# Attention and a routed expert layer on one core: weight splits in two pieces in place of eight, and four early tiles in place of three

## The chip, the cores and the metric

The kernel runs on one core of one Trainium2 chip. Its time is the device time of one execution in microseconds (us). Before the change three executions were timed. One more execution was profiled; its trace is what the profile's views are read from. A core has five engines that run their own instruction streams side by side: PE (matrix multiply), ACT and DVE (element-wise work), POOL (element-wise work and indirect transfers) and SP (which here only issues transfers). An engine's streams are tied together by semaphores: an instruction can wait until another engine has finished a certain number of its own.

## The reference

Attention comes first (8 batches, 8 heads, head size 64, 512 local and 32 global tokens), then a layer of eight experts of which each token uses one:

```python
# local tokens see local tokens within 32 positions and all 32 global ones; global tokens see all
s_ll = np.where(np.abs(pos[:, None] - pos[None, :]) <= 32, scale * q_l @ k_l.T, -1e9)
a_l = softmax(concat([scale * q_l @ k_g.T, s_ll]))
x = concat([out_g, out_l], axis=2)          # -> 8 x 544 = 4352 rows of 512
...
e_idx = np.argmax(x @ w_gate, axis=1)       # one of 8 experts a row
gate_w = softmax(x @ w_gate)[row, e_idx]
eom = sigmoid(x @ w_output_gate)
h = np.maximum(x[mask] @ w1[e], 0.0)        # w1[e]: 512 x 1024
out[mask] = gate_w * eom[mask, e] * (h @ w2[e])   # w2[e]: 1024 x 512
```

Which rows go to which expert is known only once attention has run.

## The kernel before, in words

**Attention and routing.** Units of attention pass through a pipeline (`advance`), a unit being a pair of heads for half of a batch's local tokens, or a part of its global ones. As rows become complete, a router writes each row with its gate factor and its number into a table `xd` in memory, and works out from the experts' counts a list of row numbers that is sorted by expert.

**Early tiles.** A tile is 128 rows of one expert. Expert 0's weights are loaded and split while attention still runs. So the first `KPRE` = 3 tiles of expert 0 that can be filled from the first 25 of 34 row tiles are worked on inside the tail of attention and of the routing arithmetic. `fetch_pre` gathers their rows (POOL), `turn_pre` transposes them (SP), `pre1` and `pre2` are the two matrix stages, `pre1_out` and `pre2_out` what follows them. They are cut into chunks that `work(n)` puts between other instructions; `work_all` runs those that are left, just before the expert slots.

**Expert slots.** The rest of the rows go through slots of one tile each. The number of tiles that the experts need is known only on the chip. `NBASE` = 36 slots always run (`run(0, NBASE)`); further ones stand in a tail block that is entered only if they are needed (`rest`, in steps of 2 and 3). A slot s is made of

- `gather(s)`: POOL fetches the rows (L1040), five slots ahead;
- `xtrans(s)`: a transposing DMA that SP issues (L1046), four slots ahead;
- `stage1(s)`: 96 matmuls on PE (L668), two slots ahead. Numbers are kept as sums of a high and a low half-precision part, so each product is taken as high x high, low x high and high x low, and the weights exist as `w1h` and `w1l`;
- `between(s)`: ACT takes the positive part (L674) and DVE its low part (L675);
- `stage2(s)`: 24 matmuls (L679) with `w2h` and `w2l`;
- `store(s)`: ACT scales by the gate factor (L682) and POOL scatters the rows to the output (L683).

**Changes of expert.** Where a slot is the first of a new expert, its weights, 2 MB for each matrix, must be in `w1h`/`w1l` and `w2h`/`w2l`. SP fetches the raw weights under a condition (L1012, L1014) as soon as the old raw ones are used up. Then ACT makes the high part and DVE the low part: `split1` (L693 and L695) for w1, `split2` (L699 and L701) for w2, each in eight pieces f of 512 elements a partition. Whether to do so is decided on the chip: `change` holds a Switch of two arms, one of them empty (L1019), and `changes(s)`, which runs behind each slot's stage 2, one of four (L1028): nothing, w1 for slot s + 3, w2 for slot s + 1, or both.

```python
for arm in tc.Switch(flag, 4):
    for which in (1, 2):
        if arm & which:
            for f in range(8):
                (split1 if which == 1 else split2)(f)
```

ACT and DVE each read the flag from a table, jump into an arm and come back behind the Switch. Around a Switch the count that other engines wait for must come out the same whatever arm was run, so an arm that leaves work out adds what is owed.

The order on each engine is the order in which the code is written. Nothing reorders it.

Of the kernel before, what the change touches and what calls it, by code (L numbers as in the profile page):

```python
# [21 lines left out]
S = SL + SG  # L22
# [5 lines left out]
RPE = NT  # L28
KPRE = 3
G0, G1 = (4, 7)  # L30
# [13 lines left out]
NSLOT = NT + E - 1  # L44
NBASE = NSLOT - 5
XG = DM + 8
# [12 lines left out]
def tile_attention_moe(  # L59
# [69 lines left out]
    def load_v(b, i):  # L129
        raw[i] = ld.tile([P, VW], F32, name="vf", bufs=5)  # L130
        nc.sync.dma_start(raw[i], vD[b, :, i])
# [104 lines left out]
    nc.sync.dma_start(xd[0:1, :], zrow[0:1])  # L236
    w1h = [wst.tile([P, 4, P], F16, name=f"w1h{f}") for f in range(8)]
    w1l = [wst.tile([P, 4, P], F16, name=f"w1l{f}") for f in range(8)]

# [449 lines left out]

    def split1(f, hi=True, lo=True):  # L690
        src = w1r[:, :, f * P:(f + 1) * P]
        if hi:
            nc.scalar.mul(w1h[f], src, WS)  # L693
        if lo:
            nc.vector.scalar_tensor_tensor(w1l[f], src, WS, w1h[f], ALU.mult, ALU.subtract)  # L695

    def split2(f, hi=True, lo=True):
        if hi:
            nc.scalar.mul(w2h[f], w2r[:, f], WS)  # L699
        if lo:  # L700
            nc.vector.scalar_tensor_tensor(w2l[f], w2r[:, f], WS, w2h[f], ALU.mult, ALU.subtract)  # L701

# [31 lines left out]
    def fetch_pre():  # L734
        for t in range(KPRE):
            x = ld.tile([P, XROW], F32, name="kf", bufs=3)
            gp.indirect_dma_start(out=x, out_offset=None, in_=xd[0:1 + NPRE * P, :],
                                         in_offset=bass.IndirectOffsetOnAxis(ap=ixp[:, t:t + 1], axis=0))
            pre[t] = {"x": x}
        pre_at.append(n)  # L740

    def turn_pre():
        for t in range(KPRE):
            xT = ld.tile([P, S], F32, name="qf", bufs=3).bitcast(F16)[:, 0:2 * DM].rearrange("p (k t) -> p k t", t=P)
            nc.sync.dma_start_transpose(out=xT, in_=pre[t]["x"].bitcast(F16)[:, 0:2 * DM])
            pre[t]["xT"] = xT
# [23 lines left out]
    def pre2_out(t):  # L770
        d = pre[t]
        y = ld.tile([P, VW], F32, name="vf", bufs=5)[:, 0:DM]
        s2_out(d["py"], y, d["x"])
# [242 lines left out]
    def change(s, which):  # L1016

        flag = {ET.Activation: entry(nc.scalar, 0, s), ET.DVE: entry(nc.vector, 0, s)}
        for arm in tc.Switch(flag, 2):  # L1019
            if arm == 1:  # L1020
                for f in range(8):
                    (split1 if which == 1 else split2)(f)
        fetch(s, which)

    def changes(s):

        flag = {ET.Activation: entry(nc.scalar, 4, s, 3), ET.DVE: entry(nc.vector, 4, s, 3)}
        for arm in tc.Switch(flag, 4):  # L1028
# [37 lines left out]
    def run(lo, hi, grouped=True):  # L1066

        for s in range(lo, hi):
# [13 lines left out]
            store(s, grouped)  # L1082

    for s in range(5):
        gather(s)
    for s in range(2):
        xtrans(s)
    fetch(-1, 1)
    fetch(-1, 2)
    xtrans(2)  # L1090
    for s in range(2):
        change(s, 1)
        stage1(s)
        between(s)
    xtrans(3)
    changes(-1)
    run(0, NBASE)

    def rest(lo, sizes):
# [5 lines left out]
        for arm in tc.Switch(more, 2):  # L1105
            if arm == 1:
                for s in range(lo, hi):
                    gather(s)
                for s in range(lo, hi):
                    xtrans(s)  # L1110
                for s in (lo, lo + 1):
                    change(s, 1)
                    stage1(s)
                    between(s)
                if hi > lo + 2:
                    changes(lo - 1)
                else:
                    change(lo, 2)
# [78 lines left out]
```

## Time and profile before

| | us |
|---|---|
| median of 3 runs | 746.26 (745.1 to 753.59) |
| profiled execution, its own time | 746.95 |
| its span on the core | 745.1 |
| PE busy | 686.4 (92%) |
| PE weight loads (beside PE) | 525.4 (71%) |
| DVE busy | 379.4 (51%) |
| ACT busy | 377.3 (51%) |
| POOL busy | 240.4 (32%) |

The mean clock that PE was granted is 0.974 of full speed. In the rows below, "x" ahead of a number is a count of instructions, `L668` a line of the kernel, and `out<-in` the operands by the program's names (`qkv` is the large buffer that attention used and that the expert slots use again, for raw w2, its split parts and the rows of the slots). What stands in square brackets, or behind the second bar of a group, is the time in which the engine stood idle just before the instruction, and what ended it; `ACTq` or `DVEq` is that engine's sequencer, where a branch or a count is meant and not an operation, and "issue" is a wait for nothing that the trace shows.

### The profile page before, as it was taken

To read this page: it belongs to the slowest core of one execution; us is meant where nothing else is said; L and a number is where in the kernel's file an instruction comes from. 1 tells how busy PE (TensorE), PEld (TensorE's weight loads), DVE (VectorE), ACT (ScalarE), POOL (GpSimd) and SP (SyncE) were. 2 spreads that over 40 slices of the span, in tenths; PEclk is the share of its full clock that TensorE was granted. 3 is DMA by queue.
4 is the path that set the end of the run, shared out by engine and by line. 5 is a ranking of instruction groups with operands and counts; after the bars stand their busy time and mean duration, and the time that the engine had idled before them with its cause. 6 is when DMAs were issued, how large, how long until landed. Compare 5 with 4: busy or idle time off the path is not lost.

```text
span 745.1 us, 23135 instructions
## 1 busy us (share of the span) xinstructions
PE 686.4 (92%) x9042; PEld 525.4 (71%) x9042; DVE 379.4 (51%) x1110; ACT 377.3 (51%) x866; POOL 240.4 (32%) x335
## 2 busy tenths in 40 slices
PE   4999999999999989947999899999999998999991
PEld 3788887878788777647667577667776775776660
DVE  3798989898998976710333410134225251343200
ACT  3788889898899994101342411133235262243210
POOL 3335374664748464320112121111211212121110
PEclk9999999999999999978999999999999999999996
DMA  7764979678677784297548573365765978652110
GB/s 229 226 168 127 293 213 287 148 243 208 161 236 157 208 159 75 101 264 144 168 141 221 112 149 90 81 173 124 166 189 124 238 170 212 163 113 65 49 44 14
DMA packets 113797, 120.18 MB, mean 161 GB/s; under 512 B 81615, under 2 KB 83407, under 8 KB 111762
## 3 DMA queue, kind: packets, MB, share of 16 engines
q1 hardware_dynamic: 106898, 96.85, 51.2%
q0 software_dynamic: 6528, 19.67, 9.2%
q14 instruction: 295, 2.42, 1.2%
q8 instruction: 76, 1.25, 0.7%
HBM read 200.50 MB, written 19.42 MB: 295 GB/s over the span
## 4 chain that ended last, share of the span: by engine, by line
issue 47%; PE 27%; POOL 10%; DVE 8%; ACT 4%; DMA 1%; SPq 1%; POOLq 1%; DVEq 0%; ACTq 0%
PE sp L256 6%; POOL out_dram L683 5%; POOL qkv L1040 4%; PE pt L303 3%; PE pt L308 3%; PE sp L365 2%; DVE dl L324 2%; PE sp L668 1%; DMA qkv<-in_kT_dram 1%; DVE nm L267 1%; PE pt L394 1%; DVE fl L316 1%; PE sp L261 1%; PE po L421 1%; ACT qkv L709 1%
## 5 line engine op out<-in xcount | busy, mean ns | idle before, releaser
L668 PE MATMUL ph<-qkv,w1h 128*128 128x128 f16 x2304 | 203.9, 222 | 15.1 <-DMA qkv<-qkv 10.0
L668 PEld LDWEIGHTS <-w1h 128*128 128x128 f16 x2496 | 197.0, 100 | 24.0 <-issue 10.5
L668 PE MATMUL ph<-qkv,w1l 128*128 128x128 f16 x1152 | 200.8, 222 | 9.3 <-DVEq L1028 4.1
L679 PE MATMUL py<-qkv 128*128 128x512 f16 x864 | 192.0, 379 | 0.0
L675 DVE SCALAR_TENSOR_TENSOR qkv<-ph,qkv 128x512 f16<-128x512 f32 x72 | 46.8, 687 | 213.1 <-ACT qkv L674 120.6
L679 PEld LDWEIGHTS <-qkv 128*128 128x128 f16 x896 | 86.0, 98 | 97.1
L668 PEld LDWEIGHTS <-w1l 128*128 128x128 f16 x1248 | 124.2, 99 | 10.7 <-DVEq L1028 4.6
L674 ACT ACTIVATE qkv<-ph 128x512 f16<-128x512 f32 x72 | 40.0, 594 | 167.0 <-PE ph L668 103.5
L683 POOL DMA_INDIRECT out_dram<-qkv x36 | 36.4, 1011 | 208.5 <-ACT qkv L682 207.5
L1040 POOL DMA_INDIRECT qkv<-xd,idx x36 | 36.5, 1015 | 134.7 <-DMA out_dram<-qkv 131.3
L256 PE MATMUL sp<-qkv 64*128 64x224 f32 x512 | 68.6, 388 | 9.6 <-DMA qkv<-in_kT_dram 9.6
L256 PEld LDWEIGHTS sp<-qkv 64*128 64x128 f32 x512 | 45.6, 193 | 13.5 <-issue 6.3
L285 ACT ACTIVATE p<-p,nb 128x224 f32<-128x224 f32 x128 | 51.0, 474 | 7.3 <-DVE nb L272 7.2
L682 ACT ACTIVATE qkv<-py,qkv 128x512 f32<-128x512 f32 x36 | 24.8, 689 | 58.5 <-PE py L679 39.4
L324 DVE SCALAR_TENSOR_TENSOR dl<-pt,dh 128x512 f16<-128x512 f32 x80 | 53.4, 667 | 0.3
L695 DVE SCALAR_TENSOR_TENSOR w1l<-w1r,w1h 128x512 f16<-128x512 f32 x56 | 34.3, 686 | 37.4 <-ACT w1h L693 34.7
L699 ACT ACTIVATE qkv<-qkv 128x512 f16<-128x512 f32 x56 | 34.6, 629 | 32.5 <-PE py L679 31.7
L701 DVE SCALAR_TENSOR_TENSOR qkv<-qkv 128x512 f16<-128x512 f32 x56 | 34.7, 687 | 30.8 <-ACT qkv L699 21.8
L83 POOL TENSOR_TENSOR xr<-xt,xr 128x512 f16<-128x512 f32 x30 | 34.8, 1160 | 48.0 <-ACT xr L446 36.9
L272 DVE CUSTOM_DVE_ANT_0 p<-sp,mask 128x224 f32<-128x224 f32 x128 | 42.2, 385 | 15.3 <-PE sp L256 6.2
L335 PE MATMUL po<-qkv,fh 96*128 96x65 f16 x256 | 48.1, 196 | 1.1 <-DVE s L548 0.8
L312 ACT ACTIVATE fh<-pt 96x512 f16<-96x512 f32 x64 | 37.7, 589 | 22.1 <-PE pt L303 21.5
(195 smaller groups left out, 1493.5 us busy)
## 6 DMA issues: line engine op xcount, KB each, us to landing
w1r<-in_w_dram SPq DMA_DIRECT2D x38, 2048.0 KB
qkv<-in_w_dram SPq DMA_DIRECT2D x38, 2048.0 KB
vf<-in_vD_dram SPq DMA_DIRECT2D x40, 260.0 KB
qkv<-in_kT_dram SPq DMA_DIRECT2D x7, 1280.0 KB
qkv<-in_qT_dram SPq DMA_DIRECT2D x7, 1088.0 KB
xd<-xr SPq DMA_DIRECT2D x6, 1056.0 KB
qkv<-qkv SPq DMA_DIRECT2D x14, 195.0 KB
xd<-xr SPq DMA_DIRECT2D x4, 528.0 KB
```

The source lines that it names most:

```text
L256: nc.tensor.matmul(self.sp[:, 2 * hd + bi, 0:W], lhsT=self.q[hs, pr, qs], rhs=self.k[hs, pr, ks], start=(bi == 0 or self.fused), stop=self ...
L272: nc.vector.tensor_tensor_reduce(self.p[:, n], self.sp[:, n, 0:W], mask[:, self.half + n % 2], -0.125, 3e38, ALU.add, ALU.min, self.nb[:, ...
L285: nc.scalar.activation(self.p[:, n], src, AF.Exp, bias=self.nb[:, n:n + 1], scale=sc)
L312: nc.scalar.mul(self.fh[0:96], self.pF[0:96], PS)
L324: nc.vector.scalar_tensor_tensor(self.dl, self.pD, PS, self.dh, ALU.mult, ALU.subtract)
L335: nc.tensor.matmul(o, lhsT=fh, rhs=self.vh[0:96, 4 + i, hc], start=True, stop=False)
L668: nc.tensor.matmul(o, lhsT=w[:, k], rhs=xT[:, x], start=(n == 0), stop=(n == 11))
L674: nc.scalar.activation(hh[:, gs], v, AF.Relu)
L675: nc.vector.scalar_tensor_tensor(hl[:, gs], v, 0.0, hh[:, gs], ALU.max, ALU.subtract)
L679: nc.tensor.matmul(py, lhsT=h[:, f], rhs=w, start=(f == 0 and n == 0), stop=(f == 7 and n == 2))
L683: i = nc.gpsimd.indirect_dma_start(out=out[:, :], out_offset=bass.IndirectOffsetOnAxis(ap=x[:, XG:XG + 1].bitcast(U32), axis=0), in_=y, in ...
L1040: nc.gpsimd.indirect_dma_start(out=xs, out_offset=None, in_=xd[:, :], in_offset=bass.IndirectOffsetOnAxis(ap=idx[:, s + 1:s + 2], axis=0))
```

## The change

Five things change together.

1. `split1` and `split2` work in two pieces of 2048 elements a partition in place of eight of 512. `w1h` and `w1l` become two tiles each, of four f.
2. `KPRE` is 4, so four tiles of expert 0 run early, and expert 0 has one tile fewer left for the slots. `NBASE` is 35 in place of 36 (`NSLOT - 6`), and the tail block's steps are 3 and 3.
3. The early tiles' rows lie in the tiles called `vf` (five buffers, now wide enough for a row) in place of `kf` (three), and their transposes in four `qf`.
4. At the start of the slots, `begin` puts the work in another order: both `change` Switches and both `stage1` come earlier, and slot 0's `between` stands behind the second Switch, slot 1's behind `changes(-1)`.
5. `xtrans(2)` is issued ahead of the first two weight fetches on SP. On POOL the first six gathers of the slots precede the early tiles' last two scatters; four preceded the last one before.

The diff, cut to its core:

```diff
-KPRE = 3
+KPRE = 4
...
-NBASE = NSLOT - 5
+NBASE = NSLOT - 6
...
-    w1h = [wst.tile([P, 4, P], F16, name=f"w1h{f}") for f in range(8)]
-    w1l = [wst.tile([P, 4, P], F16, name=f"w1l{f}") for f in range(8)]
+    w1hs = [wst.tile([P, 4, 4 * P], F16, name=f"w1h{g}") for g in range(2)]
+    w1ls = [wst.tile([P, 4, 4 * P], F16, name=f"w1l{g}") for g in range(2)]
+    w1h, w1l = ([t[f // 4][:, :, f % 4 * P:f % 4 * P + P] for f in range(8)] for t in (w1hs, w1ls))
...
-    def split1(f, hi=True, lo=True):
...
+    def split1(g):
+        src = w1r[:, :, g * 4 * P:(g + 1) * 4 * P]
+        nc.scalar.mul(w1hs[g], src, WS)
+        nc.vector.scalar_tensor_tensor(w1ls[g], src, WS, w1hs[g], ALU.mult, ALU.subtract)
+
+    def split2(g):
+        hi, lo = (base[0][:, at + 1024 * g:at + 1024 * g + 1024].bitcast(F16).rearrange("p (f d) -> p f d", d=DM)
+                  for at in (0, 2048))
+        src = w2r[:, 4 * g:4 * g + 4]
+        nc.scalar.mul(hi, src, WS)
+        nc.vector.scalar_tensor_tensor(lo, src, WS, hi, ALU.mult, ALU.subtract)
...
-                for f in range(8):
-                    (split1 if which == 1 else split2)(f)
+                for g in range(2):
+                    (split1 if which == 1 else split2)(g)
...
+    def begin(lo, more=True):
+
+        change(lo, 1)
+        stage1(lo)
+        change(lo + 1, 1)
+        between(lo)
+        stage1(lo + 1)
+        if lo == 0:
+            xtrans(3)
+        if more:
+            changes(lo - 1)
+        else:
+            change(lo, 2)
+        between(lo + 1)
+
     for s in range(5):
         gather(s)
-    for s in range(2):
+    for s in range(3):
         xtrans(s)
     fetch(-1, 1)
     fetch(-1, 2)
-    xtrans(2)
-    for s in range(2):
-        change(s, 1)
-        stage1(s)
-        between(s)
-    xtrans(3)
-    changes(-1)
+    begin(0)
     run(0, NBASE)
...
-    rest(NBASE, [2, 3])
+    rest(NBASE, [3, 3])
```

ACT's stream at the end of the early tiles, before (L674 is `between`'s kind of work for an early tile, L502 a router's, L682 an early tile's result):

```order
L674 ACTIVATE qkv<-sp 128x512
L502 ACTIVATE eg<-zs 128x3
L674 ACTIVATE qkv<-sp 128x512
L682 ACTIVATE vf<-pt,kf 128x512 x2
L994 TENSOR_LOAD tab
```

And after (lines from here on stand one further down: L675 is what L674 was, L683 what L682 was):

```order
L503 ACTIVATE eg<-zs 128x3
L675 ACTIVATE qkv<-sp 128x512
L683 ACTIVATE vf<-pt,vf 128x512
L675 ACTIVATE pgbuf_121<-sp 128x512 x2
L683 ACTIVATE vf<-pt,vf 128x512 x2
L994 TENSOR_LOAD tab
```

A fourth tile's two steps and its result come in between; the reading of the first flag (L994) still follows the last result.

ACT's stream at slots 0 and 1, before, from the end of slot 0's Switch to slot 1's (an unconditional branch ends an arm; the L994 rows read the flag, SWITCH_STRIDE jumps):

```order
L1193 UNCONDITIONAL_BRANCH
L674 ACTIVATE qkv<-ph_7689 128x512
L674 ACTIVATE qkv<-ph_7690 128x512
L994 TENSOR_LOAD tab
L994 ISA x2
L1193 SWITCH_STRIDE
L1193 ISA x2
L1019 BRANCH_PREFETCH_HINT
```

And after, from the reading of slot 1's flag to slot 0's `between`:

```order
L994 TENSOR_LOAD tab
L994 ISA x2
L1195 SWITCH_STRIDE
L1195 ISA x2
L1019 BRANCH_PREFETCH_HINT
L1195 UNCONDITIONAL_BRANCH
L1019 BRANCH_PREFETCH_HINT
L693 ACTIVATE w1h_163<-w1r 128x2048
L693 ACTIVATE w1h_164<-w1r 128x2048
L1195 UNCONDITIONAL_BRANCH
L675 ACTIVATE qkv<-ph_7814 128x512
L675 ACTIVATE qkv<-ph_7815 128x512
```

Slot 0's two results stood ahead of slot 1's Switch and now stand behind it; an arm holds two pieces.

DVE's arms of `changes`, before, from the end of the w1 arm through the w2 arm into the arm for both:

```order
L1193 UNCONDITIONAL_BRANCH
L1028 BRANCH_PREFETCH_HINT
L701 SCALAR_TENSOR_TENSOR qkv<-qkv 128x512 x8
L1193 UNCONDITIONAL_BRANCH
L1028 BRANCH_PREFETCH_HINT
L695 SCALAR_TENSOR_TENSOR w1l_171<-w1r,w1h_163 128x512
L695 SCALAR_TENSOR_TENSOR w1l_172<-w1r,w1h_164 128x512
```

And after, from the w1 arm to the end of the w2 arm:

```order
L1028 BRANCH_PREFETCH_HINT
L1195 UNCONDITIONAL_BRANCH
L1028 BRANCH_PREFETCH_HINT
L694 SCALAR_TENSOR_TENSOR w1l_165<-w1r,w1h_163 128x2048
L694 SCALAR_TENSOR_TENSOR w1l_166<-w1r,w1h_164 128x2048
L1195 UNCONDITIONAL_BRANCH
L1028 BRANCH_PREFETCH_HINT
L701 SCALAR_TENSOR_TENSOR qkv<-qkv 128x2048 x2
L1195 UNCONDITIONAL_BRANCH
```

Eight pieces became two of four times the length in the same arms; the four arms hold 8 splits in all, where they held 32.

More of the change, by code (lines that the diff above doesn't have):

```diff
@@ L129, in load_v @@
     def load_v(b, i):
-        raw[i] = ld.tile([P, VW], F32, name="vf", bufs=5)
+        raw[i] = ld.tile([P, XROW], F32, name="vf", bufs=5)[:, 0:VW]
         nc.sync.dma_start(raw[i], vD[b, :, i])
@@ L688, in s2_out @@
             tc.add_to_no_dep_group("out", i.ins)
-    def split1(f, hi=True, lo=True):
[L691 to L701, printed above, removed]
+    def split1(g):
[8 more added lines that the diff above has]
+        nc.vector.scalar_tensor_tensor(lo, src, WS, hi, ALU.mult, ALU.subtract)
     pre, pre_at = {}, []
@@ L735, in fetch_pre @@
         for t in range(KPRE):
-            x = ld.tile([P, XROW], F32, name="kf", bufs=3)
+            x = ld.tile([P, XROW], F32, name="vf", bufs=5)
             gp.indirect_dma_start(out=x, out_offset=None, in_=xd[0:1 + NPRE * P, :],
@@ L743, in turn_pre @@
         for t in range(KPRE):
-            xT = ld.tile([P, S], F32, name="qf", bufs=3).bitcast(F16)[:, 0:2 * DM].rearrange("p (k t) -> p k t", t=P)
+            xT = ld.tile([P, S], F32, name="qf", bufs=KPRE).bitcast(F16)[:, 0:2 * DM].rearrange("p (k t) -> p k t", t=P)
             nc.sync.dma_start_transpose(out=xT, in_=pre[t]["x"].bitcast(F16)[:, 0:2 * DM])
@@ L771, in pre2_out @@
         d = pre[t]
-        y = ld.tile([P, VW], F32, name="vf", bufs=5)[:, 0:DM]
+        y = ld.tile([P, XROW], F32, name="vf", bufs=5)[:, 0:DM]
         s2_out(d["py"], y, d["x"])
@@ L1030, in changes @@
                 if arm & which:
-                    for f in range(8):
-                        (split1 if which == 1 else split2)(f)
+                    for g in range(2):
+                        (split1 if which == 1 else split2)(g)
         fetch(s + 3, 1)
@@ L1110, in rest @@
                     xtrans(s)
[L1111 to L1118, printed above, removed]
+                begin(lo, hi > lo + 2)
                 run(lo, hi, False)
                 rest(hi, sizes[1:])
-    rest(NBASE, [2, 3])
+    rest(NBASE, [3, 3])
 def _constants():
```

## The prediction

> **What bounds the kernel now.** I read the page first, then the groups of instructions with what ended their idle time, then PE's timeline for each gap in the expert stage, then the other engines at those places.
>
> ```profile
> span 745.1 us, 23135 instructions
> PE 686.4 (92%) x9042; PEld 525.4 (71%) x9042; DVE 379.4 (51%) x1110; ACT 377.3 (51%) x866; POOL 240.4 (32%) x335
> ```
>
> PE is the bound; DVE and ACT matter only where PE stands. From 326.6 us on PE does nothing but expert tiles, and these are all its gaps there:
>
> ```profile
> 326.60 0.37 PE L668 MATMUL ph<-qkv,w1h 128*128 128x128 f16 x2 [10.00 <-DMA qkv<-qkv]
> 335.64 0.28 PE L668 MATMUL ph<-qkv,w1h 128*128 128x128 f16 x2 [1.40 <-ACTq L1019]
> 336.51 0.23 PE L668 MATMUL ph<-qkv,w1l 128*128 128x128 f16 x1 [0.59 <-DVEq L1019]
> 345.69 0.40 PE L668 MATMUL ph<-qkv,w1h 128*128 128x128 f16 x2 [3.75 <-ACTq L1028]
> 392.67 0.23 PE L668 MATMUL ph<-qkv,w1l 128*128 128x128 f16 x1 [1.76 <-DVE w1l L695]
> 403.57 0.23 PE L668 MATMUL ph<-qkv,w1l 128*128 128x128 f16 x1 [0.19 <-DVEq L1028]
> 416.89 0.29 PE L668 MATMUL ph<-qkv,w1l 128*128 128x128 f16 x1 [2.60 <-DVE qkv L701]
> 588.54 0.23 PE L668 MATMUL ph<-qkv,w1l 128*128 128x128 f16 x1 [1.23 <-DVEq L1028]
> 623.04 0.23 PE L668 MATMUL ph<-qkv,w1l 128*128 128x128 f16 x1 [2.71 <-DVEq L1028]
> 633.92 0.23 PE L668 MATMUL ph<-qkv,w1l 128*128 128x128 f16 x1 [0.16 <-DVE qkv L701]
> ```
>
> The first four are the start: 10.00 us for the first slot's transposed rows, then Switches (L1019, L1028) on ACT and DVE. The other six add to 8.65 us in 375 us, so the steady loop is nearly closed. Note the rows that name DVE L701: stage 1 reads w1 alone, yet it waits for a piece of **w2**'s low half. PE's wait is a count of DVE's finished instructions; in an arm that splits only w2, the count owed for the skipped w1 pieces comes with the first w2 piece.
>
> The granted clock after long gaps (columns: stretch, length, PE, PEld, DVE, ACT, POOL busy, clock, DMA share, GB/s):
>
> ```profile
> 326.60:331.07 4.47, 4.47 (x43) 4.47 (x44) 0.00 (x0) 0.00 (x0) 0.00 (x0) 0.50 0.97 311
> 416.40:419.80 3.40, 2.91 (x28) 2.91 (x29) 3.40 (x7) 1.66 (x3) 0.44 (x1) 0.50 0.02 5
> ```
>
> So a gap costs more than itself: 4.47/2 = 2.2 us at the start, up to 3.40/2 = 1.7 us after the 2.60 us gap.
>
> **The change, part by part.** *The tile that moves.* Counting the reference's experts, expert 0 has 665 rows, 596 of them in the first 25 tiles. Before, 36 slots follow three early tiles; now 4 x 128 = 512 rows go early and 2+3+9+5+3+3+5+5 = 35 slots follow, just the new base. PE's work is the same; a tile moves ahead of the gap at 316.6.
>
> ```profile
> 316.64 0.69 ACT L682 ACTIVATE vf<-pt,kf 128x512 f32<-128x512 f32 x1 [5.91 <-PE pt L679]
> 353.83 5.34 PE L679 MATMUL py<-qkv 128*128 128x512 f16 x24
> 385.45 5.34 PE L679 MATMUL py<-qkv 128*128 128x512 f16 x24
> ```
>
> A slot is (385.45 - 353.83)/3 = 10.54 us. From the first stage 2 on, the change saves one: **-10.5**.
>
> *The start.* Now the early tiles end at 316.64 and the first stage 2 comes at 353.83: 37.2 us that hold only three stage 1 of 5.36 (10.54 less stage 2's 686.52 - 681.34 = 5.18, rows below).
>
> ```profile
> 334.27 0.60 ACT L674 ACTIVATE qkv<-ph 128x512 f16<-128x512 f32 x1 [2.03 <-PE ph L668]
> 341.04 0.60 ACT L674 ACTIVATE qkv<-ph 128x512 f16<-128x512 f32 x1 [6.17 <-issue]
> 341.97 0.60 ACT L674 ACTIVATE qkv<-ph 128x512 f16<-128x512 f32 x1 [0.34 <-PE ph L668]
> 460.58 0.69 ACT L682 ACTIVATE qkv<-py,qkv 128x512 f32<-128x512 f32 x1 [4.63 <-PE py L679]
> 465.19 1.29 ACT L674 ACTIVATE qkv<-ph 128x512 f16<-128x512 f32 x2 [3.93 <-PE ph L668]
> 707.85 0.69 ACT L682 ACTIVATE qkv<-py,qkv 128x512 f32<-128x512 f32 x1 [4.63 <-PE py L679]
> 712.22 0.60 ACT L674 ACTIVATE qkv<-ph 128x512 f16<-128x512 f32 x1 [3.68 <-issue]
> ```
>
> A Switch lets PE go 335.64 - 334.27 = 1.37 us after ACT's last instruction before it began. Coming back out costs ACT 341.04 - 335.64 = 5.4 us with weights in flight, and 465.19 - 461.95 = 3.2 us without. Entering a far arm I price by 345.69 - 341.97 = 3.7.
>
> Now step by step. The early tiles end at 316.64 + 10.54 = 327.2. The fourth tile's result stands ahead of the first Switch on ACT, so PE starts at 327.2 + 1.37 = 328.5; the transposed rows (326.6) no longer decide, and the 10.00 us gap and its slow clock go. Stage 1 of slot 0 ends at 333.9. ACT is back at 328.5 + 5.4 and passes the second Switch at 335.2: 1.3 us late. Stage 1 of slot 1 ends at 340.6. But slot 2 is now a new expert's, where it was slot 3: `changes(-1)` must really split w1. ACT is back at 335.2 + 5.4 = 340.6, begins the second of its two results at 341.1, is in the arm at 344.8, and one piece on ACT and one on DVE (1.9 + 2.4 us, below) let PE go at 349.1, 8.5 us late. With 2.2 us of slow clock the first stage 2 begins at 349.1 + 5.3 + 2.2 = 356.6, against 353.83. With quick returns (3.2) the second Switch is in time and the same steps give 352.4. I take 355.0, nearer the slow end because both weight fetches are in flight here: **+1.2**, from -1.4 to +2.8.
>
> *Two pieces for eight.* Durations, and short forms of the same operations to scale by:
>
> ```profile
> L699 ACT ACTIVATE qkv<-qkv 128x512 f16<-128x512 f32 x56 | 34.6, 629 | 32.5 <-PE py L679 31.7
> L701 DVE SCALAR_TENSOR_TENSOR qkv<-qkv 128x512 f16<-128x512 f32 x56 | 34.7, 687 | 30.8 <-ACT qkv L699 21.8 <-issue 4.8 <-DMA qkv<-qkv 4.2
> L312 ACT ACTIVATE fh<-pt 96x512 f16<-96x512 f32 x64 | 37.7, 589 | 22.1 <-PE pt L303 21.5
> L398 ACT ACTIVATE fh<-pt 96x128 f16<-96x128 f32 x16 | 4.3, 271 | 0.4 <-PE pt L389 0.2
> L316 DVE SCALAR_TENSOR_TENSOR fl<-pt,fh 96x512 f16<-96x512 f32 x64 | 43.7, 682 | 8.3 <-ACT fh L312 8.0
> L402 DVE SCALAR_TENSOR_TENSOR fl<-pt,fh 96x128 f16<-96x128 f32 x16 | 4.5, 281 | 0.3 <-ACT fh L398 0.2
> ```
>
> ACT takes (589 - 271)/384 = 0.83 ns an element, DVE 1.04. A piece of 2048 is then an estimated 629 + 1536 x 0.83 = 1.90 us on ACT and 2.29 us on DVE. Eight small ones run in 5.09 and 5.09 us (below), two large in 3.8 and 4.6: engine time falls, but it is the first piece that PE waits for. A w2 change now:
>
> ```profile
> 681.34 1.03 PE L679 MATMUL py<-qkv 128*128 128x512 f16 x4
> 682.40 5.09 ACT L699 ACTIVATE qkv<-qkv 128x512 f16<-128x512 f32 x8 [5.48 <-PE py L679]
> 683.12 5.09 DVE L701 SCALAR_TENSOR_TENSOR qkv<-qkv 128x512 f16<-128x512 f32 x8 [7.86 <-ACT qkv L699]
> 686.52 0.28 PE L668 MATMUL ph<-qkv,w1h 128*128 128x128 f16 x2
> ```
>
> The first small piece waits for 3 of stage 2's 24 matmuls (0.65 us) and starts 1.06 after it began, 0.41 later; DVE's is done at 683.8, well before stage 1 at 686.52. A large piece waits for 12: counted from stage 2's start it begins at 2.59 + 0.41 = 3.00, ends on ACT at 4.90 and, with 0.09 between as at 683.12, on DVE at 7.28. PE needs it at 686.52 + 0.11 - 681.34 = 5.29, its third matmul, and goes on 0.06 after it (416.14 + 0.69 and 416.89 show as much), at 7.34: **2.05 us, at each of seven changes of expert, +14.4**. The second piece is done at 9.9, when PE's first half ends too, and costs nothing. The 2.60 and 0.16 us of this sort go into it: net **+11.6**, from +10 to +16 if DVE comes as late at some as at 416.89.
>
> A w1 change can start as soon as half of the last stage 1 is done, mostly in time:
>
> ```profile
> 606.09 4.27 ACT L693 ACTIVATE w1h<-w1r 128x512 f16<-128x512 f32 x8 [2.29 <-PE py L679]
> 609.63 0.22 PE L668 MATMUL ph<-qkv,w1l 128*128 128x128 f16 x1
> ```
>
> A pair of large pieces takes 1.90 + 0.09 + 2.29: from 606.09, the latest start of the five that cost nothing now, PE would stand 0.8 us; I take 1.2 for the five. Where it stood 1.76 because DVE came late it is 1.76 + 1.60 = 3.4. Together 4.6 for 1.76: **+2.8** (0 to +5). The three DVEq gaps (0.19, 1.23, 2.71) follow a w1 change, DVE being late through two branches. It leaves the arm when its last piece starts; a large one covers 2.3 us of the way back, a small one 0.7, so I let 3.0 of these 4.1 go: **-3.0** (0 to -4.1). For slow clock after gaps I take two drops against one: **+1.7** (0 to +12).
>
> *At nothing.* The fourth early gather (some 1.3 us on POOL) and transpose hide in the attention tail, where POOL still idles 2.40 us before 279.11:
>
> ```profile
> 279.11 3.51 POOL L83 TENSOR_TENSOR qkv<-qkv 128x512 f16<-128x512 f32 x3 [2.40 <-ACT qkv L709]
> 325.55 0.42 SPq L1012 DMA_DIRECT2D w1r<-in_w_dram  x1
> 331.00:335.00 4.00, 3.23 (x57) 3.06 (x54) 0.79 (x2) 1.19 (x2) 0.00 (x0) 0.99 1.03 413
> ```
>
> Without that cover they would cost about what they take, 1.3 us each. The third transpose ahead of the weight fetches puts them off by about 2 us, to 327.6; 2.1 MB at 413 GB/s land near 333 and both near 338, before ACT wants them. If not, the start reaches its slow end. Gathers ahead of results on POOL: nothing waits for those results. The other tail sizes are not entered.
>
> Sum: -10.5 + 1.2 + 11.6 + 2.8 - 3.0 + 1.7 = +3.8 us, on the profiled execution's own 746.95 (a span of 745.1 and 1.85 around it) 750.8. That execution lies 0.7 over the median of the three runs, 746.26: **750 us**. The hiding of dispatch gains about ten, and the coarse w2 piece gives it back.
>
> [...] Row first: returning over an arm with eight splits (L1019) cost 712.22 - 709.22 = 3.0 us, over arms with 32 cost 3.2. The new arms hold eight, so the sum has no gain from short jumps. [...] And the clock: half rate followed a gap of 2.60 us above. [...]
>
> **Rivals.** 1. Returns become cheap with short arms. Then PE passes slot 1 unhindered, w1's first pair starts when half of that stage 1 is through (337.0) and ends at 341.3, and the first stage 2 comes at 346.7 (-7.1); late w1 and DVEq gaps go (-1.8 - 4.1), slow clock stays as now: -7.1 - 10.5 + 11.6 - 5.9 = -11.9, **734 us**. For it: the DVEq gaps. Against: 3.0 and 3.2 above. 2. PE is not held by the first w2 piece: 3.8 - 14.4 = -10.6, **736**. For it: five of seven w2 changes show no gap now. Against: those pieces are early today, and two rows name L701. 3. Slower: each 2.1 us gap drops the clock. From eight drops in place of two come 6 x 1.7 = 10.2 us, with a start at its slow end 1.6 more: 3.8 + 11.8 = +15.6, **762**. It decides once some five of the seven do it. For it: the drop at 416.40. Against: after 2.71 us at 623.04 there was none:
>
> ```profile
> 620.00:720.00 100.00, 97.12 (x1091) 70.25 (x1089) 27.80 (x44) 31.66 (x54) 16.85 (x17) 1.00 0.43 101
> ```
>
> 4. The early tiles are not filled, 36 slots are needed, and the tail block of three runs: over 31 us, **782**. The count above speaks against it.
>
> **Chances.** Forecast 0.62, rival 1 0.10, rival 2 0.11, rival 3 0.13, rival 4 0.01, the rest unknown. The forecast's own range from its terms' ends is 743 to 758; with the first two rivals at 734 and 736 and most of the third it becomes 735 to 762. Two per cent, what a measurement here tells from no change, is 15 us: faster (under 731) needs rivals 1 and 2 at once, 0.04; slower (over 761) is most of rival 3, and 4, 0.11; same 0.85.
>
> **What would show it.** Seven PE gaps of about 2.1 us before a w1l matmul, released by DVE's w2 split; one gap of 5 to 9 us before slot 2's stage 1; no 10 us gap at 317 to 327; first stage 2 near 355. ACT pieces of 1.9 and DVE pieces of 2.3 us. Wrong would be no gap at w2 changes, ACT back from an arm in under 1 us, or a clock at 0.5 after most changes.

## The result and the profile after

The changed kernel takes 756.58 us (median of 4 runs, 755.74 to 759.36) against 745.68 before (4 runs); the ratio is 1.014, with a 95% interval of 1.010 to 1.018. So it is slower by 1.4%: clear of noise, less than the two per cent that the prediction counts as a change, and inside the forecast's range (735 to 762), but farther up than the 750 that was forecast. The profiled execution took 755.96, 1.76 of it outside the span.

The page of the changed kernel has the same work on PE in a longer span:

```profile
span 754.2 us, 22753 instructions
PE 687.7 (91%) x9042; PEld 526.9 (70%) x9042; DVE 375.5 (50%) x1026; ACT 366.4 (49%) x782; POOL 241.0 (32%) x336
```

ACT is busy 10.9 us less and DVE 3.9 less, as fewer, longer pieces should make them, and neither matters. PE's timeline shows where the time went; these are all gaps of over 0.1 us from the last early tile on, and the first stage 2 of a slot:

```profile
329.97 0.29 PE L669 MATMUL ph<-qkv,w1h 128*128 128x128 f16 x2 [1.68 <-ACTq L1019]
341.36 0.40 PE L669 MATMUL ph<-qkv,w1h 128*128 128x128 f16 x2 [5.86 <-ACTq L1019]
352.02 0.31 PE L669 MATMUL ph<-qkv,w1h 128*128 128x128 f16 x2 [3.26 <-ACT w1h L693]
354.41 0.29 PE L669 MATMUL ph<-qkv,w1l 128*128 128x128 f16 x1 [2.08 <-DVE w1l L694]
361.83 1.03 PE L680 MATMUL py<-qkv 128*128 128x512 f16 x4
379.72 0.23 PE L669 MATMUL ph<-qkv,w1l 128*128 128x128 f16 x1 [1.90 <-DVE qkv L701]
415.60 0.29 PE L669 MATMUL ph<-qkv,w1l 128*128 128x128 f16 x1 [4.09 <-DVE qkv L701]
514.81 0.23 PE L669 MATMUL ph<-qkv,w1l 128*128 128x128 f16 x1 [1.90 <-DVE qkv L701]
569.58 0.23 PE L669 MATMUL ph<-qkv,w1l 128*128 128x128 f16 x1 [1.90 <-DVE qkv L701]
603.27 0.23 PE L669 MATMUL ph<-qkv,w1l 128*128 128x128 f16 x1 [1.90 <-DVE qkv L701]
638.91 0.29 PE L669 MATMUL ph<-qkv,w1l 128*128 128x128 f16 x1 [3.85 <-DVE qkv L701]
695.27 0.23 PE L669 MATMUL ph<-qkv,w1l 128*128 128x128 f16 x1 [1.90 <-DVE qkv L701]
```

Seven gaps at seven changes of w2, each released by DVE's split of w2 (L701), five of them exactly alike; no other gap is left in the loop. At one of the five, DVE's and ACT's timelines read

```profile
562.23 1.03 PE L680 MATMUL py<-qkv 128*128 128x512 f16 x4
565.23 1.91 ACT L700 ACTIVATE qkv<-qkv 128x2048 f16<-128x2048 f32 x1 [7.43 <-PE py L680]
567.23 2.29 DVE L701 SCALAR_TENSOR_TENSOR qkv<-qkv 128x2048 f16<-128x2048 f32 x1 [10.43 <-ACT qkv L700]
```

ACT's piece starts 3.00 after stage 2 began and DVE's ends at 7.29; PE goes on at 7.35 (569.58). At 415.60 and 638.91 DVE came late to its arm as well: its pieces begin at 413.25 and 636.56, 7.2 and 7.0 us after stage 2 began, where at 567.23 it was 5.0.

The balance of the two profiled executions: the first stage 2 of a slot comes 361.83 - 353.83 = 8.0 us later. From there to the end of the span it was 745.1 - 353.83 = 391.3 and is 754.2 - 361.83 = 392.4, with one slot of 10.54 fewer: the loop lost 11.6. So 8.0 - 10.5 + 11.6 = 9.1 us, the difference of the spans.

One sentence of the description is too broad: it says that nothing reorders an engine's stream. That holds for PE, ACT, DVE and SP. The kernel fixes the order by hand for these four alone; POOL's gathers and scatters are placed by the program's scheduler, so the slots' gathers stand ahead of the early tiles' last scatters, though the code has them later.

### The profile page after: what moved, and what is told of

Same layout as the page of the kernel before. It is cut to its first block, busy times and chain, and to the rows that moved or that the text cites. A ratio compares the mean times of both kernels' runs of the same rounds, so it can differ in the third digit from the quotient of the medians.

```text
span 754.2 us, 22753 instructions
## 1 busy us (share of the span) xinstructions
PE 687.7 (91%) x9042; PEld 526.9 (70%) x9042; DVE 375.5 (50%) x1026; ACT 366.4 (49%) x782; POOL 241.0 (32%) x336
## 3 DMA queue, kind: packets, MB, share of 16 engines
q8 instruction: 76, 1.25, 0.7%
## 4 chain that ended last, share of the span: by engine, by line
issue 47%; PE 27%; POOL 9%; DVE 9%; ACT 3%; DMA 1%; SPq 1%; POOLq 1%; DVEq 0%; ACTq 0%
PE sp L257 6%; POOL out_dram L684 5%; POOL qkv L1040 4%; PE pt L304 3%; PE pt L309 3%; DVE dl L325 2%; PE sp L366 2%; DVE fl L317 1%; DMA qkv<-in_kT_dram 1%; PE sp L669 1%; DVE nm L268 1%; PE pt L395 1%; PE sp L262 1%; PE po L422 1%; PE po L424 1%
## 5 line engine op out<-in xcount | busy, mean ns | idle before, releaser
L669 PE MATMUL ph<-qkv,w1l 128*128 128x128 f16 x1120 | 197.0, 223 | 19.5 <-DVE qkv L701 17.4
L669 PE MATMUL ph<-qkv,w1h 128*128 128x128 f16 x2240 | 200.1, 223 | 10.8 <-ACTq L1019 7.5
L680 PE MATMUL py<-qkv 128*128 128x512 f16 x840 | 186.7, 379 | 0.0
L680 PEld LDWEIGHTS <-qkv 128*128 128x128 f16 x872 | 83.7, 98 | 94.5
L675 ACT ACTIVATE qkv<-ph 128x512 f16<-128x512 f32 x70 | 38.9, 595 | 148.2 <-issue 60.8
L1040 POOL DMA_INDIRECT qkv<-xd,idx x35 | 34.2, 976 | 107.3 <-DMA out_dram<-qkv 103.9
L683 ACT ACTIVATE qkv<-py,qkv 128x512 f32<-128x512 f32 x35 | 24.1, 689 | 78.6 <-PE py L680 46.1
L701 DVE SCALAR_TENSOR_TENSOR qkv<-qkv 128x2048 f16<-128x2048 f32 x14 | 31.9, 2291 | 56.9 <-ACT qkv L700 47.8
L700 ACT ACTIVATE qkv<-qkv 128x2048 f16<-128x2048 f32 x14 | 26.7, 1910 | 49.6 <-PE py L680 49.6
L694 DVE SCALAR_TENSOR_TENSOR w1l<-w1r,w1h 128x2048 f16<-128x2048 f32 x14 | 31.4, 2288 | 35.3 <-ACT w1h L693 32.4
L338 PE MATMUL po<-qkv,fl 96*128 96x65 f16 x256 | 48.1, 194 | 0.5 <-DVE fl L317 0.5
```

Of the source, the lines that this page charges most:

```text
L338: nc.tensor.matmul(o, lhsT=fl, rhs=self.vh[0:96, 4 + i, hc], start=False, stop=False)
L669: nc.tensor.matmul(o, lhsT=w[:, k], rhs=xT[:, x], start=(n == 0), stop=(n == 11))
L675: nc.scalar.activation(hh[:, gs], v, AF.Relu)
L680: nc.tensor.matmul(py, lhsT=h[:, f], rhs=w, start=(f == 0 and n == 0), stop=(f == 7 and n == 2))
L1040: nc.gpsimd.indirect_dma_start(out=xs, out_offset=None, in_=xd[:, :], in_offset=bass.IndirectOffsetOnAxis(ap=idx[:, s + 1:s + 2], axis=0))
```

## The experiments

The theory after the result has two parts. In the loop, PE's stage 1 is held by a count that comes with the w2 pieces, so their length sets the gap. At the start, three Switches on ACT lie one behind the other, where three early tiles used to leave a wait of 10 us that covered the first. The rivals: long pieces cost by themselves, ACT and DVE are late whatever the pieces, or the new order of the start is what costs. The kernel before was run again beside each group of experiments (medians 746.9 to 748.9), and each ratio is to those runs.

**Pieces alone.** The kernel before with the splits of the change, and nothing else of it:

```diff
-                for f in range(8):
-                    (split1 if which == 1 else split2)(f)
+                for g in range(2):
+                    (split1 if which == 1 else split2)(g)
```

> The kernel before with only the two pieces, for w1 and w2: three early tiles, 36 slots, the old start. Theory: the steady loop loses the same 11 us as in the changed kernel (22.5 in place of 11.3 us of delay at the changes of expert), and the first change of w1 after the start 1 to 2 us more: 758 us. Rival (the steady loop's loss needs the shifted tiles, since the arms then meet other transfers): below 752 us.

Measured: 756.34 us against 746.88, ratio 1.014 (1.005 to 1.022), within 2 us of the expectation. Four of PE's gaps at the seven w2 changes are again 1.90 us, two of them here, and all are released by the same line:

```profile
513.66 0.23 PE L669 MATMUL ph<-qkv,w1l 128*128 128x128 f16 x1 [1.90 <-DVE qkv L701]
568.44 0.23 PE L669 MATMUL ph<-qkv,w1l 128*128 128x128 f16 x1 [1.90 <-DVE qkv L701]
```

The pieces cost about what the whole change costs. Then the fourth tile must have brought next to nothing:

**Four tiles alone.** The kernel before with

```diff
-KPRE = 3
+KPRE = 4
-NBASE = NSLOT - 5
+NBASE = NSLOT - 6
-    rest(NBASE, [2, 3])
+    rest(NBASE, [3, 3])
```

and the rows in the `vf` tiles, as in the change.

> The kernel before with only the four early tiles and 35 slots: eight pieces, the old order of the start. Theory: one slot of 10.5 us goes, the steady loop keeps its 11 us of delay, and the start gets longer by some 7 us, because the Switches of slots 0, 1 and 2, which lay beside the wait for the transposed rows, now follow the early tiles: first stage 2 near 360 us, 743 us in all. Rival (it was the new order of the start that made it long): first stage 2 near 354, 737 us.

Measured: 746.79 us against 747.07, ratio 1.003 (0.999 to 1.008); the gain that was expected, 4 us, did not show in the times, which spread from 743.21 to 752.56; the span of the profiled execution is 2.4 shorter (742.7). The first stage 2 was put at 360 and is at 360.79:

```profile
340.47 0.39 PE L668 MATMUL ph<-qkv,w1h 128*128 128x128 f16 x2 [5.14 <-ACTq L1019]
352.55 0.40 PE L668 MATMUL ph<-qkv,w1h 128*128 128x128 f16 x2 [5.05 <-ACT w1h L693]
360.79 1.03 PE L679 MATMUL py<-qkv 128*128 128x512 f16 x4
```

The old order of the start, with eight pieces, has the long start too. So it comes with the fourth tile, which takes away the cover of the first Switches.

**The old order of the start** in the changed kernel:

```diff
-    begin(0)
+    for s in range(2):
+        change(s, 1)
+        stage1(s)
+        between(s)
+    xtrans(3)
+    changes(-1)
```

(and `xtrans(2)` behind the fetches).

> The changed kernel with the old order of the start (slot 0's results ahead of slot 1's Switch, the third transpose behind the weight fetches); two pieces, four tiles. Theory (the start is a chain of three Switches on ACT, whatever stands between them): within 3 us of the changed kernel, 755 to 759 us. Rival (two Switches back to back are what cost the 4.2 us jump at 337.04): 751 us.

Measured: 758.19 us, ratio to before 1.016 (1.008 to 1.025), not to be told from the changed kernel; the first stage 2 comes at 365.18. The new order is no culprit, and if anything it helps by some 3 us at the start (one profile of each).

**w2 in eight pieces, w1 in two.** In `split2`, in place of its lines for one long piece:

```diff
+        for f in range(4 * g, 4 * g + 4):
+            nc.scalar.mul(w2h[f], w2r[:, f], WS)
+            nc.vector.scalar_tensor_tensor(w2l[f], w2r[:, f], WS, w2h[f], ALU.mult, ALU.subtract)
```

> The changed kernel with w2 again split in eight pieces of 512; w1 stays in two, the early tiles and the start stay as changed. Theory (PE's stage 1 is held at a change of w2 until DVE's first w2 piece is done, so the length of that first piece sets the gap): the five gaps of 1.90 us go to nothing, and the two larger ones (4.09 and 3.85) shrink by the 1.6 us by which the first piece is shorter and by slow clock, so 22.5 us of delay become some 5: 738 us. Rival A (the gaps come from DVE and ACT leaving and entering arms late, whatever the pieces): five gaps stay near 1.9, 755 us. Rival B (the two w1 pieces are as guilty): only part comes back, 747 us.

Measured: 761.01 us, ratio 1.018 (1.009 to 1.027). The theory as I had put it failed by 23 us. **w2 in pieces of 512, 1536 and 2048**, in the same place:

```diff
+        for lo, n in ((0, 1), (1, 3)) if g == 0 else ((4, 4),):
...
+            src = w2r[:, lo:lo + n]
```

> The changed kernel with w2 in three pieces of 512, 1536 and 2048. Theory: only the first piece counts, so this runs like eight pieces, 738 us, with no gap before a w1l matmul at five of seven changes. Rival C (the number of pieces or the length of the longest counts, since the long pieces hold DVE or come too late for the next stage 2): gaps of 1 to 2 us remain, now ahead of stage 2 or of the second half of stage 1, 745 to 756 us.

Measured: 756.59 us, ratio 1.014 (1.006 to 1.023), a miss of 19 us and close to what rival C gave. PE's two largest gaps with eight pieces, and its gaps at one change with three:

```profile
418.57 0.29 PE L669 MATMUL ph<-qkv,w1l 128*128 128x128 f16 x1 [5.04 <-DVE qkv L699]
607.29 0.39 PE L669 MATMUL ph<-qkv,w1h 128*128 128x128 f16 x2 [4.69 <-ACT qkv L698]
```

```profile
511.96 0.23 PE L669 MATMUL ph<-qkv,w1l 128*128 128x128 f16 x1 [0.81 <-DVE qkv L702]
515.51 0.23 PE L669 MATMUL ph<-qkv,w1l 128*128 128x128 f16 x1 [0.70 <-DVE qkv L702]
```

With three pieces both halves of stage 1 wait; with eight, the matmuls of the high part wait as well, for ACT's w2 pieces. The cause is in the counts of the program. In the arm that splits only w1, in two pieces, the count owed for w2's n pieces is given with the first w1 piece. PE must wait for a number that holds in every arm, so it waits for n + 1 and, in its second half, for n + 2. In the arm that splits only w2, where the owed 2 come with the first piece, those numbers are reached by the last but one w2 piece and by the last. With two pieces of each, and with eight of each, that is the first piece; with 2 and 8 it is the seventh of eight, with 2 and 3 the second of three. The traces agree: PE goes on at 418.57, 0.06 us after DVE's seventh piece of eight ends, and at 511.96 and 515.51, 0.06 us after its second and its third of three. "PE waits for the first w2 piece" holds only where both matrices are cut alike.

**The count given early.** The changed kernel's two pieces stay as long as they are; tiny copies of one column on ACT and DVE make the counts come out otherwise:

```diff
+            if arm == 2:
+                small(1)
             for which in (1, 2):
...
+            if arm == 1:
+                small(2)
```

> The changed kernel with its two pieces of 2048, and one tiny copy on ACT and one on DVE ahead of the w2 pieces in the arm that splits only w2 (and two tiny copies on each behind the w1 pieces in the arm that splits only w1), so that the count that stage 1 waits for is reached before the first w2 piece. Theory: the five gaps of 1.90 us go although every piece is as long as before, and the two large ones lose the 2.3 us of the piece and keep DVE's lateness (some 1.8 each, and slow clock at one at most): 737 to 740 us. Rival A or C (the long pieces themselves, or lateness, cost the time): 754 to 757 us.

Measured: 751.13 us, ratio 1.006 (1.002 to 1.009). From first stage 2 to end, PE has these gaps:

```profile
392.81 0.29 PE L669 MATMUL ph<-qkv,w1l 128*128 128x128 f16 x1 [3.73 <-DVE w1l L694]
578.24 0.23 PE L669 MATMUL ph<-qkv,w1l 128*128 128x128 f16 x1 [3.62 <-DVE w1l L694]
592.94 0.23 PE L669 MATMUL ph<-qkv,w1l 128*128 128x128 f16 x1 [2.36 <-DVEq L1035]
618.55 0.29 PE L669 MATMUL ph<-qkv,w1l 128*128 128x128 f16 x1 [4.35 <-DVE w1l L694]
```

All seven w2 gaps are gone with pieces of 2048, so the count is their cause and not the length as such, and rival C falls with it. But of the 17 us expected only 5 to 6 arrived. In the place of the w2 gaps stand gaps at changes of w1, 14.1 us in all, where the changed kernel has none. DVE's timeline around the second, in this kernel and then in the changed one:

```profile
568.79 1.29 DVE L676 SCALAR_TENSOR_TENSOR qkv<-ph,qkv 128x512 f16<-128x512 f32 x2 [0.51 <-issue]
575.89 4.49 DVE L694 SCALAR_TENSOR_TENSOR w1l<-w1r,w1h 128x2048 f16<-128x2048 f32 x2 [5.81 <-issue]
```

```profile
572.72 1.29 DVE L676 SCALAR_TENSOR_TENSOR qkv<-ph,qkv 128x512 f16<-128x512 f32 x2 [0.74 <-issue]
576.93 4.49 DVE L694 SCALAR_TENSOR_TENSOR w1l<-w1r,w1h 128x2048 f16<-128x2048 f32 x2 [2.93 <-issue]
```

An expert of three slots has its w2 change and the next expert's w1 change in successive slots. In the changed kernel the stall lies between the two and gives DVE two microseconds more. That is the smaller part. The larger is DVE's jump into the w1 arm, here and then in the changed kernel (the columns are the stretch, its length, the busy time of PE, PEld, DVE, ACT and POOL, the clock, the DMA share and GB/s):

```profile
569.75:575.71 5.96, 4.87 (x25) 2.16 (x22) 0.33 (x1) 3.98 (x4) 0.00 (x0) 1.00 0.91 295
```

```profile
573.67:576.68 3.01, 3.01 (x33) 2.04 (x31) 0.33 (x1) 2.71 (x2) 0.98 (x1) 1.00 0.51 155
```

At the two other such changes the jump took 6.12 and 6.54 us here, beside 288 to 293 GB/s, and 2.91 in the changed kernel, beside 120 to 146. The fetch of the next w2 was issued 0.13 us after DVE's last w2 piece here (568.42) and 1.77 us after it there (573.74), so here its transfers ran beside the jump. So this run shows that the w2 gaps hang on the count; how much of the w1 gaps comes from the missing stall alone it does not show.

**Four pieces for both** in the changed kernel:

```diff
-                for g in range(2):
+                for g in range(4):
...
-        src = w2r[:, 4 * g:4 * g + 4]
+        src = w2r[:, 2 * g:2 * g + 2]
```

> The changed kernel with both matrices in four pieces of 1024. Estimates from the measured pieces: 1.05 us on ACT and 1.22 on DVE, so the first w2 piece is done on DVE some 4.1 us after stage 2 began, and PE wants it at 5.3. Theory: no gap at the five w2 changes where DVE is in time. Since taking those gaps away alone brought gaps before w1 pieces of 2.4 to 4.4 us, part comes back as those: 22.5 us of delay become some 11, as with eight pieces before, 745 us. Rival (any long piece costs): still 1.9 us gaps, 755 us.

Measured: 748.70 us, ratio 1.001 (0.997 to 1.005). The five 1.90 us gaps are gone, which settles the rival "any long piece". Part came back as expected, though more of it: five gaps of 2.2 to 4.1 us, 14.1 in all, at two changes of w1 and at three of w2. By time four pieces can't be told from eight with the same tiles (746.79).

**Without the first two Switches.** In `begin(0)` of the changed kernel:

```diff
-        change(lo, 1)
+        if lo:
+            change(lo, 1)
+        else:
+            fetch(lo, 1)
         stage1(lo)
-        change(lo + 1, 1)
...
+            fetch(lo + 1, 1)
```

> The changed kernel without the Switches of slots 0 and 1, so without the split of w1 there; for these data both slots go on with expert 0 and would run the empty arm. Theory (the start is bound by ACT's jumps into and out of arms): the 5.86 us gap before slot 1's stage 1 and most of the slow clock behind it go, the one before slot 2 stays; first stage 2 near 349 in place of 361.8, 743 us. Rival (the start is bound by the weight fetches or the transposed rows): first stage 2 not before 358, 752 us or more.

Measured: 747.23 us against 743 expected, ratio 0.997 (0.993 to 1.002). The first stage 2 comes at 353.19, 8.6 us earlier than in the changed kernel, and not at 349. ACT's timeline shows what is left:

```profile
334.80 0.60 ACT L675 ACTIVATE qkv<-ph 128x512 f16<-128x512 f32 x1 [2.03 <-PE ph L669]
341.19 3.71 ACT L693 ACTIVATE w1h<-w1r 128x2048 f16<-128x2048 f32 x2 [5.80 <-issue]
```

and in the changed kernel:

```profile
350.06 3.71 ACT L693 ACTIVATE w1h<-w1r 128x2048 f16<-128x2048 f32 x2 [2.79 <-issue]
```

ACT stood 5.80 us before slot 2's first piece here and 2.79 there; the jump alone took 5.24 here, beside 391 GB/s, and 2.83 there, beside 12. It has no fixed price.

**Slot 0's Switch beside the early tiles.** With eight pieces and four tiles, this stands ahead of the last two early tiles' second stages; slot 0's `between` goes behind `changes(-1)`:

```diff
+    for s in range(5):
+        gather(s)
+    for s in range(3):
+        xtrans(s)
+    fetch(-1, 1)
+    fetch(-1, 2)
+    change(0, 1)
     work_all()
```

> Four early tiles, eight pieces for both matrices, and a new start: slot 0's gathers, transposes, weight fetches and its Switch stand ahead of the last two early tiles' second stages, and the first two slots' results stand behind the third Switch. Theory (a jump into an arm costs some 4 us where the engine left the last arm under 1 us before, and 0.4 where that was long ago; ACT needs 5 to 6 us to come back): slot 0's Switch is over while PE still works on early tiles, slot 1's is passed before slot 0's stage 1 ends, and only the gap before slot 2 stays; first stage 2 near 352 in place of 360.8, and 738 us against the 746.8 of four tiles with eight pieces. Rival (weight fetches or transposed rows come late, or ACT's long way back delays the early tiles' results): first stage 2 near 358 and 744 us or more.

Measured: 739.55 us against 747.73, ratio 0.990 (0.986 to 0.994). This is faster than both kernels, by 1% over the one before. The same start with **four pieces**:

> The same start with both matrices in four pieces of 1024. Theory: the start gains the same 8 to 9 us on the 748.7 of four pieces: 740 us, 1 to 3 us behind eight pieces, whose changes of expert leave some 12 us of delay against 19. Rival (with shorter arms the way back is shorter): equal to eight pieces or ahead.

Measured: 743.56 us, ratio 0.996 (0.993 to 0.999), 4 us behind eight pieces. The first stage 2 of the eight-piece kernel comes at 357.0, not at the 352 expected and near the 358 of the rival; that is 3.8 us earlier than with four tiles and the old start, about half of the 7 us by which the medians differ. PE's gaps at its start:

```profile
329.38 0.27 PE L668 MATMUL ph<-qkv,w1h 128*128 128x128 f16 x2 [0.82 <-ACT vf L682]
335.19 0.28 PE L668 MATMUL ph<-qkv,w1h 128*128 128x128 f16 x2 [0.29 <-ACTq L1011]
348.70 0.40 PE L668 MATMUL ph<-qkv,w1h 128*128 128x128 f16 x2 [7.89 <-ACT w1h L693]
```

The gaps before slots 0 and 1 are nearly closed, the one before slot 2 grew to 7.89.

**Without the first weight fetches.** The eight-piece kernel with the new start, less two lines:

```diff
-    fetch(-1, 1)
-    fetch(-1, 2)
     change(0, 1)
```

> The kernel with eight pieces and slot 0's Switch ahead of the last early stages, without the first two weight fetches: expert 1's slots multiply with expert 0's weights, and 4 MB of transfers are missing at the start. Theory (a jump between arms waits for code that comes by DMA, and 4 MB at 400 GB/s are in its way): ACT's jumps at slots 1 and 2, 5.6 and 6.0 us with the fetches, fall to 3 or less, the gap of 7.9 us before slot 2's stage 1 to some 2, and the first stage 2 comes near 350 in place of 357.0; 733 us. Rival (a jump soon after another costs this much whatever is in flight): first stage 2 stays near 357, 739 us.

Measured: 734.87 us, ratio 0.983 (0.977 to 0.989), and the first stage 2 at 349.23. The trace records when ACT takes a branch and when its next instruction runs. With those times as borders, the windows of three kernels are, for ACT's jump at slot 1, its way back, and its jump into slot 2's w1 arm (columns as above). The eight-piece kernel with the fetches:

```profile
329.44:335.10 5.66, 5.46 (x96) 5.29 (x95) 0.00 (x0) 0.00 (x0) 0.98 (x1) 1.00 1.02 248
335.10:341.78 6.68, 5.61 (x96) 5.37 (x96) 0.00 (x0) 0.00 (x0) 0.00 (x0) 1.00 1.03 403
341.78:347.80 6.02, 0.00 (x0) 0.00 (x0) 0.00 (x0) 0.00 (x0) 0.00 (x0) 0.66 1.31 244
```

Without them (its second row is the way back alone; above, that row holds 0.9 us more):

```profile
329.59:334.15 4.56, 4.56 (x84) 4.56 (x84) 0.00 (x0) 0.00 (x0) 0.98 (x1) 1.00 0.95 227
334.30:337.46 3.16, 2.32 (x43) 2.14 (x40) 0.00 (x0) 0.00 (x0) 0.00 (x0) 1.00 0.04 10
338.50:341.62 3.12, 2.91 (x53) 2.73 (x49) 0.00 (x0) 0.00 (x0) 0.00 (x0) 1.00 0.24 57
```

The changed kernel's jump at slot 1, and its jump at slot 2:

```profile
337.04:341.22 4.18, 0.00 (x0) 0.00 (x0) 0.00 (x0) 0.00 (x0) 0.00 (x0) 0.67 1.03 391
346.99:349.82 2.83, 1.78 (x32) 1.60 (x29) 1.11 (x2) 0.27 (x1) 0.00 (x0) 1.00 0.04 12
```

In these rows a jump or a way back takes 4.2 to 6 us beside 227 to 403 GB/s, and 2.8 to 3.2 beside 57 or less. Taking the fetches away shortened the last two to about half (6.02 to 3.12 us for slot 2's jump), which shows that the transfers are a cause. ACT's other ways back in the changed kernel's slots go the same way: ten beside under 60 GB/s took 2.4 to 3.2 us, nine beside over 300 took 5.5 to 6.5. Slot 1's jump, which fell among other transfers of 227 GB/s, shrank only to 4.56, against an expectation of 3. Transfers do not settle its price: with four pieces, and all fetches, it took 2.33 beside 252 GB/s. In the changed kernel's trace one DMA packet of the kind `instruction` begins in slot 1's jump, among 784 of the queue that carries the weights; in slot 2's three do, and no others. Which engine these are for, whether the jump waits for them, and how transfers lengthen it no run here shows.

**The w2 fetch later.** In the eight-piece kernel with the new start:

```diff
-    fetch(-1, 2)
...
         if lo == 0:
             xtrans(3)
+            fetch(-1, 2)
```

> The kernel with eight pieces and slot 0's Switch ahead of the last early stages, with the first w2 fetch issued behind the fourth transpose, so that it starts some 5 us later. Theory as for the run without fetches: slot 1's jump falls among fewer transfers, slot 2's among as many or more; first stage 2 within 3 us of 357.0, 737 to 741 us. Rival (jumps cost the same whatever is in flight): 739.5, no difference.

Measured: 740.33 us, ratio 0.989 (0.984 to 0.994): no difference in time from 739.55, which the theory and its rival both allow. The first stage 2 begins at 352.58, 4.4 us earlier, but it stops after two matmuls:

```profile
352.58 0.59 PE L679 MATMUL py<-qkv 128*128 128x512 f16 x2
355.03 4.92 PE L679 MATMUL py<-qkv 128*128 128x512 f16 x22 [1.85 <-DVE qkv L675]
```

It ends at 359.95 against 362.35, 2.4 us earlier. The jump into slot 2's arm, expected beside as many transfers or more, fell beside 41 GB/s and took 2.67 us in place of 6.00; slot 1's took 2.18 beside 263 GB/s in place of 5.61. The loop was slower in the profile by more than the start gained (gaps of up to 3.70 us at late w2 splits); why stays open.

## Why the prediction was right, and where not

- **The slot saved, -10.5.** Right: 32 slots of 10.54 lie between first and last stage 2's, one fewer than before.
- **The w2 stall, net +11.6 (+10 to +16).** Right in mechanism and size. Pieces of 1.91 and 2.29 us stood against the estimates of 1.90 and 2.29, ACT's start and DVE's end came at 3.00 and 7.29 after stage 2 began, against 3.00 and 7.28. The seven gaps add to 17.4, less the 2.76 of before: +14.7, above the forecast's value because two were longer, as the range allowed. Each 1.90 us gap made its slot 2.07 longer, near the 2.05 forecast. The reason given, that the count comes "with the first w2 piece", holds only for equal numbers of pieces. I carried the shortened sentence into two experiments and they missed.
- **w1, +2.8, and the DVEq gaps, -3.0.** Both too dear: none of either is left, -1.8 and -4.1. That DVE "leaves the arm when its last piece starts" the traces show at changes of w2 (before, its branch at 687.53 and the piece at 687.52), not at those of w1, which the DVEq gaps follow: there the branch stood 0.63 to 3.03 us ahead of the last piece's start before, and 0.38 to 1.42 in the changed kernel. The terms were summed as if they stood alone. That PE's stall at w2 gives DVE the time for w1 is argued, not shown: the run with the early count has the w1 gaps, but DVE's jumps are 3 us longer there.
- **Slow clock, +1.7.** The rest of the loop's 11.6 is 11.6 - 14.7 + 1.8 + 4.1 = 2.8, from slow clock and the span's end. In windows of the changed kernel the clock fell at the two long gaps and not at a 1.90 us one, and at the four others of 1.90 it did not fall either, which decides against rival 3:

```profile
412.00:424.00 12.00, 8.40 (x98) 7.93 (x99) 6.42 (x6) 4.34 (x6) 3.60 (x2) 0.72 0.31 94
566.00:576.00 10.00, 8.10 (x110) 6.52 (x108) 5.87 (x4) 6.75 (x7) 1.96 (x2) 1.00 0.11 27
636.00:646.00 10.00, 7.09 (x96) 6.97 (x97) 5.69 (x4) 3.33 (x6) 3.06 (x2) 0.83 0.22 68
```

- **The start, +1.2 (-1.4 to +2.8): the step that failed; it was +8.0.** "ACT is back at 328.5 + 5.4 and passes the second Switch at 335.2: 1.3 us late." The price of passing a Switch, 1.37 us, came from a Switch that ACT reached 16 us after its last branch. Here it came straight from another arm, with weights in flight, and the jump alone took 4.18 us: PE stood 5.86. Against the slow end of the range, 356.6, the start was off by 5.2: PE began 1.5 later (329.97; the early tiles' last result came at 328.38, not 327.2, of which more below), +4.6 for slot 1's Switch, -3.2 for slot 2's gap (3.26 + 2.08 in place of 8.5), and +2.4 for slow clock, since the three stage 1 fill 361.83 - 329.97 = 31.9 us with 16.1 of work at full clock and 11.2 of gaps. That I took 355.0 and not 356.6 is the rest.
- **At nothing.** The fourth gather was not hidden. From 269 us to a routing step's matmuls near 313, PE took 43.31 us in both kernels with three early tiles (the one before, and the pieces alone), and 43.96 to 44.94 in all twelve with four; the changed kernel has 43.96, so 0.65 of its 1.2 us. PE's gaps near 272 grew from 0.91 and 0.82 to one of 2.70. There the fourth gather (POOL, 269.17) puts POOL's next operations off by 1.25 us, and a DVE operation of 0.16 us, before and after, ends only with POOL's at 273.65:

```profile
270.86 0.16 DVE L516 TENSOR_TENSOR ohsum<-ohsum,os 128x8 bf16<-128x8 bf16 x1
271.44 2.24 DVE L517 TENSOR_TENSOR ohsum<-ohsum,os 128x8 bf16<-128x8 bf16 x1
```

  The rest of the 1.2 us was there ahead of 269, where the kernels do the same work and the profiles differ by up to 1.3 either way. PE never waits for the transposed rows now. The weight fetches, put at nothing if they land in time, did land in time, but a jump beside them took longer: slot 2's 6.02 us with them and 3.12 without, in the eight-piece kernel with the new start.
- **The rivals.** Cheap returns from short arms: no; ACT's ways back at slots 0 and 1 took 6.3 and 4.7 us with two pieces, and 5.4 at slot 1 with eight before. PE not held by w2: no. A clock drop at each gap: no. Tail block: not entered.

The forecast was thus too low by one term of 6.8 us, less 1.5 by which the loop was put too dear. That the loop came so near is luck in part: its terms were off by +3.1 (w2), -4.6 (w1), -1.1 (DVEq) and +1.1 (clock), and these cancel. The start lies outside its own bounds; the total is inside 743 to 758, the range from the terms alone, because the loop's errors stand against it. Its sentence that "the hiding of dispatch gains about ten, and the coarse w2 piece gives it back" held for the pieces, but at the start most of the ten was lost a second time.

## What to carry to other kernels

A wait on a shared count ties the reader to whatever instruction brings the count to that number (with w1 in two pieces and w2 in eight PE went on 0.06 us after the seventh w2 piece): before a piece is made longer, work out for every arm of a branch which piece that is. A jump priced where the engine had long been back from the last arm (ACT's into an empty arm took 0.43 to 0.44 us there) is no price for one that soon follows another jump (1.2 to 1.4 us, and 3.6 to 4.8 beside 245 GB/s or more); so dispatch that lay beside a wait must be priced anew when the wait goes, and it is better moved (ahead of the last early work: 739.6 us against 746.8 with the same tiles and pieces) than uncovered. Removing a stall moves what comes behind it, transfers too: where the count came early, the next weights' fetch fell beside DVE's next jump (5.96 us in place of 3.01), and gaps of 14.1 us at changes of w1 took most of what had been won.

## What was not expected of the hardware

In the changed kernel ACT's jump into an empty arm took 0.43 to 0.44 us at all thirteen slots where ACT had been back from the last arm for 2.6 us or more, one of them beside 327 GB/s. Where it had been back for 0.8 to 1.1 us, it took 1.2 to 1.4 beside 6 GB/s or less (five slots) and 3.6 to 4.8 beside 245 to 391 GB/s (four). With slot 0's Switch early, slot 1's jump took 2.2 to 5.6 us though ACT had been back for 2.6 to 3.2, beside 227 to 263 GB/s; this stays open.

The number of splits in the arms, 8 or 32 in all, made no difference that the ways back show: beside under 60 GB/s they took 2.4 to 3.2 us in the changed kernel and 2.5 to 3.0 before, beside over 300 GB/s 5.5 to 6.5 and 5.4 to 6.5.

The clock does not follow the length of PE's gap alone. From 362 us on, over all fourteen traces, no gap of 1.90 to 1.94 us (21) has a stretch at half clock beside it, all of 3.39 us and more (15) have one, and of 22 between 1.97 and 3.21 us 12 have. The stretches lasted 3.41 or 6.83 us.
